# Transposing q and k by DMA from staging rows that already hold the mask columns, in an attention plus gated feed-forward kernel

## The chip, the cores and the metric

One core of one Trainium2 chip. The time is the device time of one execution in microseconds, the median of several runs; the spans inside the profile are some 2 us shorter. A run is called fast when it shows no sign of the chip's slower state. Comparisons inside one set of runs were made on the same chip.

Names used below: PE is the matrix engine; VectorE, ScalarE and GpSimd are the other engines that compute; SyncE issues DMA transfers. SBUF is the on-chip memory that tiles live in, PSUM the memory that PE's results land in, and copying a result from PSUM to SBUF is called an eviction. A staging buffer holds rows that wait to be transposed; a gate is a tiny copy that makes a load wait for something else.

## The reference, cut to what matters

Four batches, eight heads, 768 tokens, head width 64, then a feed-forward with a beta-scaled gate:

```python
scores = (q @ k.T) / sqrt(64)                       # per batch and head, 768 x 768
mask   = |bi - bj| <= 1 or bi, bj in {0, 23} or bj in sampled_blocks[bi]   # blocks of 32 tokens
attn   = softmax(where(mask, scores, -1e9))
x      = (attn @ v), heads side by side             # 3072 tokens x 512
h      = x @ w_in                                   # 512 -> 2048
out    = (h * sigmoid(beta * h)) @ w_out            # 2048 -> 512
```

PE wants q and k with the head width on partitions, that is transposed: 16 pairs of heads, a q and a k each.

The block mask costs no pass of its own. Each transposed k carries 24 extra rows, the one-hot number of the token's block; each transposed q carries 24 rows with 0 or -30000 for every block that it may not see. The score matmul then adds the mask by itself.

## The kernel before

The parts that the change and the argument touch; cuts are marked.

```python
# persistent transposed tiles, five sets; the two heads of a pair lie in different halves
for i in range(NSET):                                # NSET = 5
    for nm in ("kA", "qA", "kB", "qB"):
        four[nm] = persist.tile([P, S], FP16)        # P = 128, S = 768
    nc.gpsimd.memset(four["kB"][0:D, :], 0.0)
    nc.gpsimd.memset(four["qB"][0:D, :], 0.0)
# ... cut ...
def emit_set(i):                                     # mask rows of a set, once each
    nc.vector.tensor_copy(out=four["qA"][D:D + NB, :], in_=maskx)
    nc.gpsimd.tensor_copy(out=four["kA"][D:D + NB, :], in_=oh_flat)
    nc.vector.tensor_copy(out=four["qB"][0:NB, :], in_=maskx)
    nc.gpsimd.tensor_copy(out=four["kB"][0:NB, :], in_=oh_flat)

def emit_prep(b, j):                                 # one pair of heads
    for name, st32 in (("k", kst), ("q", qst)):
        st16 = stage_pool.tile([P, NC, 2, D], FP16, bufs=2)
        nc.vector.tensor_copy(out=st16, in_=st32)    # fp32 -> fp16 (views cut)
        tp = mm_pool.tile([P, NC, P], FP16)          # PSUM, pool of 3 shared with h and out
        for c in range(NC):                          # NC = 6
            nc.tensor.transpose(out=tp[:, c, :], in_=st16[:, c], identity=identity)
        nc.vector.tensor_copy(out=four[f"{name}A"][0:D, :], in_=flat[0:D, :])
        nc.vector.tensor_copy(out=four[f"{name}B"][D:P, :], in_=flat[D:P, :])
    nc.vector.tensor_copy(out=va[:, :, :, 0:D], in_=vst)
# ... cut ...
if n_loaded[0] == 3:                                 # the weights start once pair 3's k is loaded
    gate(w_in_sb, loaded[seq[3]][0])
    for i in range(4): emit_w_in(i)                  # 8 loads on GpSimd's queue, 8.4 MB in HBM
    for i in range(4): emit_w_out(i)
```

Attention works in query tiles of 256 or 512 columns; each step is six score matmuls, an exponential on ScalarE, then attention times v. The feed-forward of the tile before is woven in between. The first tile (256 columns) has no such filling.

The softmax here doesn't subtract the row's maximum and nothing guards it: scores larger than these inputs give would overflow.

## Time and profile before

| | before |
|---|---|
| time, median | 339.52 us (339.43 to 339.88) |
| PE busy | 298.4 of 337.4 us |
| VectorE busy | 181.7 us |
| first score matmul | 21.7 us |
| first 512-wide score matmul (second query tile) | 48.4 us |

The page of the kernel before. The first line shown is busy time by engine with instruction counts; the rows after it cut the span in 40 slices, each digit a busy share in tenths; the last line is the DMA queue fed by SyncE, with packets, MB and its share of 16 DMA engines' time.

```profile
PE 298.4 (88%) x2659; PEld 172.2 (51%) x2659; DVE 181.7 (54%) x408; ACT 215.8 (64%) x297; POOL 28.0 (8%) x48
...
PE   0055589999999999999999999999999999999995
...
DVE  3989764543787451557866366115667114561360
...
PEclk9999999999999999999999999999999999999999
DMA  7999994112530340021340000011000010001101
...
q1 hardware_dynamic: 16512, 25.17, 21.8%
```

PE is full from the seventh slice on. The slices before that are the ramp, where VectorE and DMA are the full ones. Here is the ramp's second half and the rest, as busy time in windows (the last three columns are the clock granted to PE, the DMA share and GB/s; a DMA share over 1 comes from packets that overlap on an engine):

```profile
core 0: us, PE busy (x) PEld busy (x) DVE busy (x) ACT busy (x) POOL busy (x), PEclk, DMA share, GB/s
22.00:40.00 18.00, 8.53 (x68) 6.36 (x67) 17.35 (x38) 3.77 (x6) 7.11 (x7) 1.00 1.20 239
48.00:338.00 290.00, 278.72 (x2486) 157.13 (x2483) 144.97 (x335) 203.43 (x282) 0.00 (x0) 1.00 0.17 58
```

VectorE is busy 17.35 of 18 us in the ramp and half of the time after it. Four landmarks from the timeline of the kernel before (start, duration, engine, line, operation, out<-in):

```profile
21.69 1.49 PE L234 MATMUL sc<-qA_137,kA_136 88*128 88x256 f16 x6
...
44.88 0.50 PE L209 MATMUL tp<-identity,k_479 128*128 128x128 f16 x6
...
45.22 0.50 PE L209 MATMUL tp<-identity,q_490 128*128 128x128 f16 x6
...
45.55 0.88 PE L234 MATMUL sc<-qA_155,kA_154 88*128 88x256 f16 x6
...
48.39 0.38 PE L234 MATMUL sc<-qA_137,kA_136 88*128 88x512 f16 x1 [0.26 <-ACT et L240]
```

The 12 transposes of a pair hold PE from 44.88 to 45.55, about 0.7 us. The first 512-wide score matmul at 48.39 ends the ramp; from there to the end of the span is 289.0 us. I use these two parts, ramp and rest.

### The profile page before, as it was taken

The numbers are of one execution on the slowest core, as the hardware profiler recorded it, in microseconds if no ns is written. First come the engines' busy times: TensorE is split into PE (matmuls) and PEld (weight loads), VectorE is DVE, ScalarE is ACT, GpSimd is POOL, SyncE is SP. The second block draws the span as 40 slices with busy tenths as digits, with TensorE's granted clock in tenths as the row PEclk, the third lists the DMA queues.
The fourth block names the chain that finished last, engine by engine and source line by source line (L and its number), as shares of the span: only waits on it lengthen the run. The fifth ranks groups of instructions, "written<-read, shape, count | busy, mean of one in ns | idle before, by whom it ended". The sixth has DMA issues, their size and how long they took to land.

```text
span 337.4 us, 6399 instructions
## 1 busy us (share of the span) xinstructions
PE 298.4 (88%) x2659; PEld 172.2 (51%) x2659; DVE 181.7 (54%) x408; ACT 215.8 (64%) x297; POOL 28.0 (8%) x48
## 2 busy tenths in 40 slices
PE   0055589999999999999999999999999999999995
PEld 0034466655555555555566445455455455555662
DVE  3989764543787451557866366115667114561360
ACT  1011389985998545978554989665986756954561
POOL 9994000000000000000000000000000000000000
PEclk9999999999999999999999999999999999999999
DMA  7999994112530340021340000011000010001101
GB/s 242 384 228 225 267 330 179 50 47 80 161 97 11 123 130 33 31 79 64 96 157 31 33 0 2 31 38 58 1 3 0 33 62 33 0 2 62 64 2 62
DMA packets 20880, 29.78 MB, mean 88 GB/s; under 512 B 1380, under 2 KB 17780, under 8 KB 20852
## 3 DMA queue, kind: packets, MB, share of 16 engines
q1 hardware_dynamic: 16512, 25.17, 21.8%
q0 software_dynamic: 4224, 4.19, 7.5%
q8 instruction: 21, 0.34, 0.4%
q14 instruction: 7, 0.06, 0.1%
q10 hardware_dynamic: 116, 0.01, 0.0%
HBM read 27.27 MB, written 6.29 MB: 99 GB/s over the span
## 4 chain that ended last, share of the span: by engine, by line
PE 64%; DVE 16%; ACT 14%; issue 4%; DMA 2%; SPq 0%; ACTq 0%; DVEq 0%
PE op L313 23%; PE hp L294 16%; PE sc L234 12%; PE av L260 9%; ACT et L240 8%; ACT t_sb L299 6%; DVE g L301 4%; PE tp L209 2%; PE xtp L274 2%; DMA qst<-in_q_dram 2%; DVE q_203 L204 1%; DVE va_70 L217 0%; DVE xst L266 0%; DVE qB_157 L214 0%; DVE qB_139 L214 0%
## 5 line engine op out<-in xcount | busy, mean ns | idle before, releaser
L240 ACT ACTIVATE et<-sc 128x1024 f16<-128x1024 f32 (+1 forms) x160 | 146.8, 953 | 80.4 <-PE sc L234 80.2
L313 PE MATMUL op<-w_out_sb,g 128*128 128x512 f16 x384 | 97.0, 379 | 0.1
L294 PE MATMUL hp<-xT_sb,w_in_sb 128*128 128x512 f16 (+1 forms) x448 | 95.6, 348 | 1.0 <-DVE g L301 0.2
L301 DVE SCALAR_TENSOR_TENSOR g<-t_sb,hp 128x512 f16<-128x512 f16 (+1 forms) x112 | 67.1, 610 | 44.9 <-ACT t_sb L299 44.4
L299 ACT ACTIVATE t_sb<-hp,beta_h_sb 128x512 f16<-128x512 f32 (+1 forms) x112 | 69.8, 653 | 12.1 <-PE hp L294 10.9
L294 PEld LDWEIGHTS <-w_in_sb 128*128 128x128 f16 x448 | 42.2, 97 | 35.9 <-issue 1.9
L260 PEld LDWEIGHTS <-et 128*128 128x128 f16 x1152 | 44.2, 99 | 21.6 <-DVE xst L266 10.4
L313 PEld LDWEIGHTS <-g 128*128 128x128 f16 x384 | 34.9, 97 | 33.2 <-DVE qB_163 L214 0.4
L265 DVE RECIPROCAL recip<-av 128x2 f32<-128x2 f32 (+1 forms) x64 | 11.2, 176 | 70.3 <-PE av L260 70.0
L318 ACT ACTIVATE osb<-op 128x512 f32<-128x512 f32 x24 | 14.3, 598 | 23.2 <-PE op L313 19.7
L266 DVE TENSOR_TENSOR xst<-av,recip 128x128 f16<-128x128 f32 (+1 forms) x64 | 22.8, 357 | 1.6
L276 DVE COPY xT_sb<-xtp 128x256 f16<-128x256 f16 (+1 forms) x32 | 11.5, 358 | 14.6 <-PE xtp L274 14.6
L274 PEld LDWEIGHTS <-xst 128*128 128x128 f16 x96 | 6.4, 97 | 12.5 <-DVE xst L266 12.2
L260 PE MATMUL av<-va_70,et 128*128 128x65 f16 x216 | 9.6, 199 | 2.8 <-DVE xst L266 2.7
L234 PE MATMUL sc<-qB_139,kB_138 128*128 128x256 f16 (+1 forms) x48 | 11.6, 344 | 0.5 <-ACT et L240 0.5
L274 PE MATMUL xtp<-identity,xst 128*128 128x128 f16 x96 | 10.9, 222 | 1.0 <-DVE xst L266 0.9
L234 PE MATMUL sc<-qA_137,kA_136 88*128 88x256 f16 (+1 forms) x48 | 11.1, 344 | 0.5 <-ACT et L240 0.3
L180 PE MATMUL mkx<-onehot,mask_121 24*24 24x512 f16 (+1 forms) x2 | 0.8, 506 | 10.3 <-DVE mask_121 L126 10.3
L260 PE MATMUL av<-va_72,et 128*128 128x65 f16 x216 | 9.5, 196 | 0.0
L234 PE MATMUL sc<-qB_145,kB_144 128*128 128x256 f16 (+1 forms) x36 | 8.8, 348 | 0.9 <-ACT et L240 0.9
L234 PE MATMUL sc<-qA_143,kA_142 88*128 88x256 f16 (+1 forms) x36 | 8.7, 350 | 0.6 <-ACT et L240 0.6
L234 PE MATMUL sc<-qB_163,kB_162 128*128 128x512 f16 (+1 forms) x36 | 8.5, 325 | 0.7 <-ACT et L240 0.7
(206 smaller groups left out, 249.4 us busy)
## 6 DMA issues: line engine op xcount, KB each, us to landing
kst<-in_k_dram SPq DMA_DIRECT2D x16, 384.0 KB, 4.7
qst<-in_q_dram SPq DMA_DIRECT2D x16, 384.0 KB, 5.5
vst<-in_v_dram SPq DMA_DIRECT2D x16, 384.0 KB, 5.4
out_dram<-osb SPq DMA_DIRECT2D x24, 256.0 KB, 2.0
w_in_sb<-in_moe_w_in_dram POOLq DMA_DIRECT2D x4, 512.0 KB, 10.1
w_out_sb<-in_moe_w_out_dram POOLq DMA_DIRECT2D x4, 512.0 KB, 21.7
sb_i_95<-in_sampled_blocks_dram ACTq DMA_DIRECT2D x1, 0.3 KB
beta_sb<-in_moe_beta_dram ACTq DMA_DIRECT2D x1, 8.0 KB, 4.5
```

The source lines that it names most:

```text
L234: nc.tensor.matmul(sc[:, i * n:(i + 1) * n], lhsT=kx[0:rows, (kc0 + i) * P:(kc0 + i + 1) * P], rhs=qx[0:rows, q0:q0 + n], start=True, stop ...
L240: nc.scalar.activation(out=et[:, 0:kn * n], in_=sc[:, 0:kn * n], func=AF.Exp, bias=0.0, scale=SCALE)
L260: nc.tensor.matmul(av[:, qc, :], lhsT=et[:, i * n + qc * P:i * n + (qc + 1) * P], rhs=va[:, hh, kc, 0:D + 1], start=(kc == 0), stop=(kc == ...
L265: nc.vector.reciprocal(out=recip[:, 0:nq], in_=av[:, 0:nq, D])
L266: nc.vector.tensor_tensor(out=xstage[:, 0:nq, hh * D:(hh + 1) * D], in0=av[:, 0:nq, 0:D], in1=recip[:, 0:nq].to_broadcast([P, nq, D]), op= ...
L274: nc.tensor.transpose(out=xtp[:, qc, :], in_=xstage[:, qc, :], identity=identity)
L276: nc.vector.tensor_copy(out=xT_sb[:, j, b * S + q0:b * S + q0 + n], in_=xtp[:, 0:nq, :].rearrange("p c s -> p (c s)"))
L294: nc.tensor.matmul(hp[:, 0:n], lhsT=w_in_sb[:, c, f * P:(f + 1) * P], rhs=xT_sb[:, c, t0:t0 + n], start=(c == 0), stop=(c == NPAIR - 1))
L299: nc.scalar.activation(out=t_sb[:, 0:n], in_=hp[:, 0:n], func=AF.Tanh, bias=0.0, scale=beta_h_sb[:, f:f + 1])
L301: nc.vector.scalar_tensor_tensor(out=g[:, f, 0:n], in0=t_sb[:, 0:n], scalar=1.0, in1=hp[:, 0:n], op0=ALU.add, op1=ALU.mult)
L313: nc.tensor.matmul(op, lhsT=g[:, f, ts * P:(ts + 1) * P], rhs=w_out_sb[:, f, :], start=(f == 0), stop=(f == N_FFC - 1))
L318: nc.scalar.activation(out=osb, in_=op, func=AF.Copy, bias=0.0, scale=0.5)
```

## The change

The intent: let the DMA engines transpose q and k, so that PE loses 192 transposes and VectorE 64 evictions. The staging rows (tokens on partitions) now hold 128 columns a head: 64 of data, 24 of mask or one-hot, the rest zero. The columns are written once, by ScalarE, into two staging buffers each for k and q; a DMA transpose then yields data and mask rows together. The mask chain and the loads of pair 1 were moved forward in the program.

```diff
-    et_pool = ctx.enter_context(tc.tile_pool(name="et", bufs=14))
+    et_pool = ctx.enter_context(tc.tile_pool(name="et", bufs=13))
-    NVA = 6
+    NVA = 5
+    NSTG = 2
+    AUG = P - D
+    for nm in ("k", "q"):
+        stg[nm] = [persist.tile([P, 2, NC, P], FP16, name=f"{nm}stg_{i}") for i in range(NSTG)]
@@ emit_load for pair 1 goes to ScalarE's queue; one-hot in token order (cut) @@
+    def emit_mask():
+        ps = mm_pool.tile([P, NC, AUG], FP32, tag="mm", name="mkt")
+        for c in range(NC):
+            nc.tensor.matmul(ps[:, c, :], lhsT=oh_flat[:, c * P:(c + 1) * P], rhs=mask16,
+                             start=True, stop=True)
+        for i in range(NSTG):
+            for h in range(2):
+                nc.scalar.copy(out=stg["k"][i][:, h, :, D:P], in_=oh_tok)
+                nc.scalar.copy(out=stg["q"][i][:, h, :, D:P], in_=ps)
@@ emit_set, the zero fills and the four half tiles of a set are gone (cut) @@
-            nc.vector.tensor_copy(...)               # cast into a pool tile
-            for c in range(NC):
-                nc.tensor.transpose(...)
-            nc.vector.tensor_copy(...)               # two evictions
+            st16 = stg[name][n_prep[0] % NSTG]
+            nc.vector.tensor_copy(out=st16[:, :, :, 0:D],
+                                  in_=st32.rearrange("p h (c d) -> p h c d", d=D))
+            nc.sync.dma_start_transpose(
+                out=dst.rearrange("p h (c s) -> p (h c) s", s=P),
+                in_=st16.rearrange("p h c e -> p (h c e)"))
```

More of the change, by code (lines that the diff above doesn't have):

```diff
@@ L47 @@
     stage_pool = ctx.enter_context(tc.tile_pool(name="stage", bufs=3))
-    et_pool = ctx.enter_context(tc.tile_pool(name="et", bufs=14))
+    et_pool = ctx.enter_context(tc.tile_pool(name="et", bufs=13))
     work_pool = ctx.enter_context(tc.tile_pool(name="work", bufs=3))
     g_pool = ctx.enter_context(tc.tile_pool(name="g", bufs=2))
-    NVA = 6
+    NVA = 5
+    NSTG = 2
+    AUG = P - D
     va_tiles = []
     for i in range(NVA):
-        va = persist.tile([P, 2, NC, VW], FP16, name=f"va_{i}")
-        nc.gpsimd.memset(va[:, :, :, D:VW], 1.0)
-        va_tiles.append(va)
+        va_tiles.append(persist.tile([P, 2, NC, VW], FP16, name=f"va_{i}"))
+    stg = {}
+    for nm in ("k", "q"):
+        stg[nm] = [persist.tile([P, 2, NC, P], FP16, name=f"{nm}stg_{i}") for i in range(NSTG)]
     def pair_src(x, b, j):
@@ L63, with emit_load @@
     loaded = {}
-    def emit_load(b, j):
+    def emit_load(b, j, eng=None):
+        eng = eng or nc.sync
         sts = []
@@ L68, in emit_load @@
             st32 = stage_pool.tile([P, 2, NC * D], FP32, tag=f"{name}st", name=f"{name}st")
-            nc.sync.dma_start(out=st32, in_=pair_src(src, b, j))
+            eng.dma_start(out=st32, in_=pair_src(src, b, j))
             sts.append(st32)
@@ L73 @@
     identity = persist.tile([P, P], FP16, name="identity")
+    ident32 = persist.tile([16, 16], FP32, name="ident32")
     emit_load(0, 0)
-    make_identity(nc, identity)
-    ident32 = persist.tile([P, P], FP32, name="ident32")
-    nc.gpsimd.tensor_copy(out=ident32[0:16, 0:16], in_=identity[0:16, 0:16])
     sb_i32 = persist.tile([NB, 3], mybir.dt.int32, name="sb_i32")
@@ L86 @@
     beta_sb = persist.tile([N_FFC, P], FP32, name="beta_sb")
+    emit_load(0, 1, nc.scalar)
     nc.scalar.dma_start(out=beta_sb, in_=moe_beta.rearrange("(c p) -> c p", p=P))
@@ L110 @@
                             channel_multiplier=BLK)
+    oh_tok = persist.tile([P, NC, AUG], FP16, name="oh_tok")
+    nc.gpsimd.memset(oh_tok, 1.0)
+    nc.gpsimd.affine_select(out=oh_tok, in_=oh_tok, pattern=[[1, NC], [-BLK, AUG]],
+                            compare_op=ALU.is_ge, fill=0.0, base=0,
+                            channel_multiplier=NC)
+    nc.gpsimd.affine_select(out=oh_tok, in_=oh_tok, pattern=[[-1, NC], [BLK, AUG]],
+                            compare_op=ALU.is_ge, fill=0.0, base=BLK - 1,
+                            channel_multiplier=-NC)
+    mask16 = persist.tile([NB, AUG], FP16, name="mask16")
+    nc.gpsimd.memset(mask16, 0.0)
+    for va in va_tiles:
+        nc.gpsimd.memset(va[:, :, :, D:VW], 1.0)
+    make_identity(nc, identity)
+    nc.gpsimd.tensor_copy(out=ident32, in_=identity[0:16, 0:16])
     mask_blk = persist.tile([NB, NB], FP32, name="mask_blk")
@@ L124 @@
                                        in1=mask_blk, op0=ALU.is_equal, op1=ALU.max)
-    mask16 = persist.tile([NB, NB], FP16, name="mask16")
-    nc.vector.tensor_scalar(out=mask16, in0=mask_blk, scalar1=1.0, scalar2=-NEG,
+    nc.vector.tensor_scalar(out=mask16[:, 0:NB], in0=mask_blk, scalar1=1.0, scalar2=-NEG,
                             op0=ALU.subtract, op1=ALU.mult)
@@ L162, with emit_beta @@
     for i in range(NSET):
-        four = {}
-        for nm in ("kA", "qA", "kB", "qB"):
-            four[nm] = persist.tile([P, S], FP16, name=f"{nm}_{i}")
-        nc.gpsimd.memset(four["kB"][0:D, :], 0.0)
-        nc.gpsimd.memset(four["qB"][0:D, :], 0.0)
-        sets.append(four)
-    maskx_box = {}
-    def emit_mask():
+        sets.append((persist.tile([P, 2, S], FP16, name=f"kX_{i}"),
+                     persist.tile([P, 2, S], FP16, name=f"qX_{i}")))
+    def emit_mask():
+        ps = mm_pool.tile([P, NC, AUG], FP32, tag="mm", name="mkt")
[6 more added lines that the diff above has]
+                nc.scalar.copy(out=stg["q"][i][:, h, :, D:P], in_=ps)
+    def emit_beta():
         ps = mm_pool.tile([P, 512], FP32, tag="mm", name="bet")
-        nc.tensor.transpose(out=ps[:, 0:N_FFC], in_=beta_sb, identity=ident32[0:16, 0:16])
+        nc.tensor.transpose(out=ps[:, 0:N_FFC], in_=beta_sb, identity=ident32)
         nc.vector.tensor_scalar(out=beta_h_sb, in0=ps[:, 0:N_FFC], scalar1=0.5,
                                 scalar2=None, op0=ALU.mult)
-        maskx = persist.tile([NB, S], FP16, name="maskx")
-        for lo, hi in ((0, 512), (512, S)):
-            ps = mm_pool.tile([P, 512], FP32, tag="mm", name="mkx")
-            nc.tensor.matmul(ps[0:NB, 0:hi - lo], lhsT=mask16, rhs=oh_flat[:, lo:hi],
-                             start=True, stop=True)
-            nc.vector.tensor_copy(out=maskx[:, lo:hi], in_=ps[0:NB, 0:hi - lo])
-        maskx_box["m"] = maskx
-    def emit_set(i):
-        four, maskx = sets[i], maskx_box["m"]
-        nc.vector.tensor_copy(out=four["qA"][D:D + NB, :], in_=maskx)
-        nc.gpsimd.tensor_copy(out=four["kA"][D:D + NB, :], in_=oh_flat)
-        nc.vector.tensor_copy(out=four["qB"][0:NB, :], in_=maskx)
-        nc.gpsimd.tensor_copy(out=four["kB"][0:NB, :], in_=oh_flat)
     prepared = {}
@@ L197, in emit_prep @@
         kst, qst, vst = loaded.pop((b, j))
-        four = sets[n_prep[0] % NSET]
-        if n_prep[0] < NSET:
-            emit_set(n_prep[0])
-        for name, st32 in (("k", kst), ("q", qst)):
-            st16 = stage_pool.tile([P, NC, 2, D], FP16, tag=f"{name}16", name=f"{name}16",
-                                   bufs=2)
-            nc.vector.tensor_copy(
-                out=st16.rearrange("p c h d -> p h c d"),
-                in_=st32.rearrange("p h (c d) -> p h c d", d=D))
-            tp = mm_pool.tile([P, NC, P], FP16, tag="mm", name="tp")
-            for c in range(NC):
-                nc.tensor.transpose(out=tp[:, c, :],
-                                    in_=st16[:, c, :, :].rearrange("p h d -> p (h d)"),
-                                    identity=identity)
-            flat = tp.rearrange("p c s -> p (c s)")
-            nc.vector.tensor_copy(out=four[f"{name}A"][0:D, :], in_=flat[0:D, :])
-            nc.vector.tensor_copy(out=four[f"{name}B"][D:P, :], in_=flat[D:P, :])
+        kX, qX = sets[n_prep[0] % NSET]
+        for name, st32, dst in (("k", kst, kX), ("q", qst, qX)):
+            st16 = stg[name][n_prep[0] % NSTG]
[4 more added lines that the diff above has]
+                in_=st16.rearrange("p h c e -> p (h c e)"))
         va = va_tiles[n_prep[0] % NVA]
@@ L218, in emit_prep @@
                               in_=vst.rearrange("p h (c d) -> p h c d", d=D))
-        prepared[(b, j)] = (four, va)
+        prepared[(b, j)] = (kX, qX, va)
     def attn_steps(b, j, q0, n):
@@ L228, in run @@
             def run():
-                four, _ = prepared[(b, j)]
-                kx, qx = (four["kA"], four["qA"]) if hh == 0 else (four["kB"], four["qB"])
-                rows = D + NB if hh == 0 else P
+                kX, qX, _ = prepared[(b, j)]
                 sc = sc_pool.tile([P, 1024], FP32, tag="sc", name="sc")
@@ L235, in run @@
                         sc[:, i * n:(i + 1) * n],
-                        lhsT=kx[0:rows, (kc0 + i) * P:(kc0 + i + 1) * P],
-                        rhs=qx[0:rows, q0:q0 + n],
+                        lhsT=kX[0:D + NB, hh, (kc0 + i) * P:(kc0 + i + 1) * P],
+                        rhs=qX[0:D + NB, hh, q0:q0 + n],
                         start=True, stop=True)
@@ L251, in run @@
             def run():
-                _, va = prepared[(b, j)]
+                _, _, va = prepared[(b, j)]
                 if hh == 0:
@@ L332 @@
     seq = [(b, j) for b in range(B) for j in range(NPAIR)]
-    n_loaded, n_prepped = [1], [0]
+    n_loaded, n_prepped = [2], [0]
     def prep_upto(i):
@@ L351 @@
     prep_upto(0)
+    emit_beta()
     backlog = []
```

## The prediction

> **What bounds it now.** The page shows PE busy 298.4 of 337.4 us, at full granted clock. Two stages:
> - 0 to 48 us, the ramp. By the timeline the first score matmul starts at 21.7 us, the first 512-wide one (second query tile) at 48.4. From 22 to 40 us VectorE is busy 17.35 of 18 us (windows), PE 8.5, ScalarE 3.8: VectorE binds, with casts, mask copies (24 rows, ten, 5.3 us in all) and the evictions of transposed q and k (64x768, 0.55 us, four a pair).
> - 48 us to the end: PE is busy over 98% of most windows, with 512-column matmuls at 0.86 us per four, near its rate. Every PE instruction removed here is worth its issue time.
>
> **Removed.** 192 PE transposes: 12 of one pair took 0.7 us in the warm stage (44.8 to 45.5); 12 pairs are left after 44 us, about 8.6 us; the chain of waits puts 6.1 us (1.8%) on them. VectorE: 64 evictions, 35.5 us, two thirds of it in slack, 11 in the ramp; mask copies, 5.3. GpSimd: 8 us of zero fills, 9.9 us of one-hot copies. The shared PSUM pool (3 buffers) loses the transposes' tiles, which held up h matmuls: perhaps 1 us.
>
> **Added.** 32 DMA transposes of 384 KB (128 x 1536, fp16), all on the SP queue; eight ScalarE copies at the start. No duration in this trace fits the transpose. The Trainium skill, "DMA: Bandwidth & Descriptors", section "Latency and other measured facts", gives 261 GB/s for one: my estimate is 1.5 us of transfer; with latency I take 2 to 3 us each, 4 or more beside other loads. No trace here shows it. After 55 us DMA is about a third busy or less, and q and k are prepared well ahead, so transposes should hide.
>
> **The ramp decides the size.** DMA moves 225 to 385 GB/s until 55 us already (page, part 2). The order of instructions puts the mask chain on VectorE behind six casts of pairs 0 and 1 and one of pair 2's v; so despite the intent I expect the mask at 14 us, its copies at 15 to 17, and the first transpose issued at 16 to 17, behind loads of pairs 2 to 4 on SP's queue. First score matmul: 21 to 24 us, no gain. Then eight transposes of pairs 0 to 3, between loads and 4 MB of weights, at about 2.5 us each: pair 3 ready near 40 us, the second tile starting at 42 to 46 instead of 48.4. The transpose stream binds, no longer VectorE.
>
> **Sum.** 339.5 - 8.6 (PE transposes) - 1 (PSUM pool) - 3 (ramp) = about 327; I put 328 for contention. Range 316 to 341. Faster by over 2%: 0.62; within 2%: 0.24; slower by over 2%: 0.14.
>
> **What would show each step.**
> - PE: busy falls by 12 to 17 us, 192 fewer matmuls.
> - VectorE: busy from 182 to about 140; GpSimd from 28 to about 10, ending before 15 us.
> - From 48 us on: the same work takes 8 to 10 us less, PE never idle for a transpose.
> - Transposes: median 2 to 5 us from issue to landing.
> - Ramp: first score matmul at 21 to 24 us; score matmuls wait on transposes, not on VectorE.
>
> **What would make it wrong.** At 5 us or more of exclusive queue time a transpose, eight in the ramp cost 40 us and the ramp grows by about 10 us, against the 8.6 gained: "same". At 10 us or more, 32 of them would bind the kernel: much slower. Under 1.5 us, the ramp ends before 40 us and the time is under 320. In SP's fixed order, a late transpose also holds back the loads and stores behind it.

## The result, and the profile after

The changed kernel takes 364.45 us (362.23 to 365.91, four runs) against 339.56 (four runs beside it): a ratio of 1.0726 (1.0668 to 1.0784), slower by 7%. A ratio here is the mean time of one kernel's fast runs over that of the other's fast runs of the same rounds, so it is not quite the ratio of the medians that I quote.

The page of the changed kernel, the same lines:

```profile
PE 295.1 (82%) x2471; PEld 164.7 (46%) x2471; DVE 136.1 (38%) x332; ACT 220.2 (61%) x305; POOL 11.8 (3%) x31
...
PE   0000187979797999998989998999999999999995
...
DVE  1600043345324552135682236622255312661270
...
PEclk9999999987998999998999999999999999999999
DMA  7999999998996000019992104325100011001101
...
q1 hardware_dynamic: 65872, 36.58, 41.1%
```

The work went away as planned: VectorE from 181.7 to 136.1 us, GpSimd from 28.0 to 11.8. But PE is empty for four slices instead of two, has gaps until past the middle of the span, and, unlike before, its clock dips below full. The DMA row is full about twice as long. Now the ramp in the timeline of the changed kernel; SPq is SyncE's queue, and the duration there is how long it took to issue:

```profile
18.14 4.87 SPq L210 DMA_TRANSPOSE kX_149<-kstg_75  x1
...
23.11 9.39 SPq L210 DMA_TRANSPOSE qX_150<-qstg_77  x1
32.60 9.03 SPq L210 DMA_TRANSPOSE kX_151<-kstg_76  x1
...
41.71 3.92 SPq L210 DMA_TRANSPOSE qX_152<-qstg_78  x1
...
43.24 1.44 PE L230 MATMUL sc<-qX_150,kX_149 88*128 88x256 f16 x6 [24.78 <-DMA qX_150<-qstg_77]
...
64.59 1.47 PE L230 MATMUL sc<-qX_150,kX_149 88*128 88x512 f16 x3
```

The first score matmul comes at 43.2 instead of 21.7 us, after 24.8 us of idle time of PE that ended when one transpose landed, q of pair 0. The second tile starts at 64.6 instead of 48.4: the ramp is 16.2 us longer. From there to the end is 360.5 - 64.6 = 295.9 us, against 289.0: 6.9 us longer, although the PE transposes of 11 pairs, which the kernel before still does after its second tile has started, are gone. The two add up to the 23.1 us by which the span grew. So there are two losses to explain.

Windows of the changed kernel: the ramp, and 8 us of the stage after it.

```profile
core 0: us, PE busy (x) PEld busy (x) DVE busy (x) ACT busy (x) POOL busy (x), PEclk, DMA share, GB/s
22.00:40.00 18.00, 0.00 (x0) 0.11 (x1) 0.56 (x1) 0.00 (x0) 0.52 (x1) 1.00 1.22 196
...
76.00:80.00 4.00, 1.85 (x27) 0.96 (x24) 2.36 (x7) 3.60 (x6) 0.00 (x0) 0.89 0.77 233
80.00:84.00 4.00, 4.00 (x20) 2.61 (x19) 1.47 (x4) 1.95 (x4) 0.00 (x0) 0.50 0.65 229
```

From 22 to 40 us the engines do almost nothing; only DMA works, and it moves 196 GB/s at a full share, against 239 before. At 76 us PE stalls, and then its clock is at half for the next 4 us. The chain of waits of the changed kernel around that stall (start, us, what):

```profile
72.06 5.49 DMA kX_149<-kstg_76
...
77.64 0.56 DVE kstg_76 L208
78.20 0.66 DVE g L297 x2
```

And VectorE's timeline there:

```profile
74.89 0.42 DVE L262 TENSOR_TENSOR xst<-av,recip 128x256 f16<-128x256 f32 x1
77.64 0.56 DVE L208 CAST kstg_76<-kst 128x768 f16<-128x768 f32 x1 [2.33 <-DMA kX_149<-kstg_76]
```

A cast into staging buffer 76 waits 2.33 us for the transpose that still reads that buffer. Nothing needs this cast soon: it belongs to a later pair. But VectorE takes its instructions in order, so the gate product (g), the reciprocal and the normalisation behind it wait too. PE runs out of work and its clock falls.

### The profile page after: what moved, and what is told of

Same layout as the page of the kernel before. It is cut to its first block, busy times and chain, and to the rows that moved or that the text cites. A ratio compares the mean times of both kernels' runs of the same rounds, so it can differ in the third digit from the quotient of the medians.

```text
span 360.5 us, 6016 instructions
## 1 busy us (share of the span) xinstructions
PE 295.1 (82%) x2471; PEld 164.7 (46%) x2471; DVE 136.1 (38%) x332; ACT 220.2 (61%) x305; POOL 11.8 (3%) x31
## 3 DMA queue, kind: packets, MB, share of 16 engines
q1 hardware_dynamic: 65872, 36.58, 41.1%
## 4 chain that ended last, share of the span: by engine, by line
PE 58%; DMA 20%; ACT 9%; DVE 7%; issue 3%; SPq 1%; ACTq 1%; DVEq 0%
PE op L309 20%; PE hp L290 16%; PE sc L230 13%; DMA qX_150<-qstg_77 7%; PE av L256 7%; ACT et L236 5%; DMA vst<-in_v_dram 4%; DVE g L297 3%; ACT t_sb L295 3%; DMA qX_156<-qstg_78 3%; PE xtp L270 2%; DMA kX_149<-kstg_76 2%; DMA kX_155<-kstg_75 2%; DMA qX_154<-qstg_78 1%; SPq L210 1%
## 5 line engine op out<-in xcount | busy, mean ns | idle before, releaser
L290 PE MATMUL hp<-xT_sb,w_in_sb 128*128 128x512 f16 (+1 forms) x448 | 99.8, 361 | 0.8 <-DVE g L297 0.2
L290 PEld LDWEIGHTS <-w_in_sb 128*128 128x128 f16 x448 | 44.3, 101 | 39.0 <-issue 5.5
L256 PEld LDWEIGHTS <-et 128*128 128x128 f16 x1152 | 46.4, 100 | 23.9 <-DVE xst L262 14.3
L230 PE MATMUL sc<-qX_150,kX_149 88*128 88x256 f16 (+1 forms) x96 | 23.7, 358 | 25.1 <-DMA qX_150<-qstg_77 24.8
L230 PEld LDWEIGHTS <-kX_149 88*128 88x128 f16 x96 | 9.6, 105 | 32.6 <-DMA kX_149<-kstg_75 14.9
L230 PE MATMUL sc<-qX_152,kX_151 88*128 88x256 f16 (+1 forms) x72 | 17.9, 358 | 2.9 <-ACT et L236 1.8
L230 PE MATMUL sc<-qX_154,kX_153 88*128 88x256 f16 (+1 forms) x72 | 18.0, 361 | 0.8 <-ACT et L236 0.8
L270 PE MATMUL xtp<-identity,xst 128*128 128x128 f16 x96 | 11.8, 237 | 7.7 <-DVE xst L262 7.7
L230 PE MATMUL sc<-qX_156,kX_155 88*128 88x256 f16 (+1 forms) x72 | 17.5, 349 | 0.4 <-ACT et L236 0.3
L272 DVE COPY xT_sb<-xtp 128x256 f16<-128x256 f16 (+1 forms) x32 | 11.5, 358 | 14.5 <-PE xtp L270 14.5
L230 PE MATMUL sc<-qX_158,kX_157 88*128 88x512 f16 (+1 forms) x72 | 16.4, 332 | 0.2 <-ACT et L236 0.2
L186 PE MATMUL mkt<-mask_113,onehot 24*128 24x64 f16 x6 | 0.5, 231 | 16.7 <-DVE mask_113 L145 16.7
L256 PE MATMUL av<-va_70,et 128*128 128x65 f16 x288 | 13.2, 198 | 0.6 <-DVE xst L262 0.6
```

The costliest lines, as they stand in the source:

```text
L230: nc.tensor.matmul(sc[:, i * n:(i + 1) * n], lhsT=kX[0:D + NB, hh, (kc0 + i) * P:(kc0 + i + 1) * P], rhs=qX[0:D + NB, hh, q0:q0 + n], star ...
L256: nc.tensor.matmul(av[:, qc, :], lhsT=et[:, i * n + qc * P:i * n + (qc + 1) * P], rhs=va[:, hh, kc, 0:D + 1], start=(kc == 0), stop=(kc == ...
L270: nc.tensor.transpose(out=xtp[:, qc, :], in_=xstage[:, qc, :], identity=identity)
L272: nc.vector.tensor_copy(out=xT_sb[:, j, b * S + q0:b * S + q0 + n], in_=xtp[:, 0:nq, :].rearrange("p c s -> p (c s)"))
L290: nc.tensor.matmul(hp[:, 0:n], lhsT=w_in_sb[:, c, f * P:(f + 1) * P], rhs=xT_sb[:, c, t0:t0 + n], start=(c == 0), stop=(c == NPAIR - 1))
```

## The experiments

The two theories. **Ramp:** the transposes are late because they share the 16 DMA engines with the eight weight loads, and lose (A); rival: a transpose is slow by itself (B). **After it:** VectorE's queue behind a cast that waits for a transpose (C); rival: the DMA traffic itself slows the engines (D).

### e1: the weights wait

```diff
-                if n_loaded[0] == 3:
-                    gate(w_in_sb, loaded[seq[3]][0])
             emit_prep(*seq[x])
+            if x == 3:       # one 1x1 GpSimd copy from pair 3's transposed q before each of the 8 loads
+                for i in range(4):
+                    nc.gpsimd.tensor_copy(out=w_in_sb[0:1, 0, i*512:i*512+1], in_=last[0:1, 0, 0:1])
+                    emit_w_in(i)         # and the same for w_out
```

> Changed kernel, but each of the eight weight loads waits until pair 3's q is transposed. Theory A (the ramp grew because the first transposes share the 16 DMA engines with 8 weight loads): kX and qX of pair 0 land within 10 us of the first issue at about 18 us, first score matmul at 25 to 29 us instead of 43.2; the time falls by 8 to 18 us unless the late weights hold up the first h matmuls. Rival B (a transpose is slow by itself, 10 us or more of queue): first score matmul still after 38 us, time unchanged or worse.

Measured: 361.29 us (358.76 to 362.59). The timeline of this run has its two landmarks:

```profile
23.22 1.44 PE L230 MATMUL sc<-qX,kX 88*128 88x256 f16 x6 [6.66 <-DMA qX<-qstg]
...
43.69 1.47 PE L230 MATMUL sc<-qX,kX 88*128 88x512 f16 x3
```

The first score matmul came at 23.2 us (a little before the range), the second tile at 43.7 us, 4.7 us before that of the kernel before. So A holds and B falls: the same two transposes, the first issued at 17.4 us, were done in under 6 us without the weights, and the first four were issued at most 1.9 us apart. But the time fell by 3 us instead of the 8 to 18 expected. The chain of waits of this run shows where the gain went:

```profile
42.39 15.56 DMA qX<-qstg
...
61.24 15.49 DMA kX<-kstg
```

The collision moved with the weights, from pairs 0 and 1 to pairs 4 and 5. These two transposes are not needed for a long while, yet each of them held a VectorE cast: the waits view of 43 to 95 us has 13.1 us of VectorE waiting for kX and 10.6 us for qX, and PE did nothing from 68 to 76 us. That is mechanism C with a late transpose of 15 us instead of 5. From the second tile to the end this run took 315.9 us.

### e2: casts on GpSimd after the ramp

```diff
-            nc.vector.tensor_copy(out=st16[:, :, :, 0:D], ...)
+            eng = nc.vector if n_prep[0] < 4 else nc.gpsimd
+            eng.tensor_copy(out=st16[:, :, :, 0:D], ...)
```

> Changed kernel, but from pair 4 on the q and k casts into the two staging buffers run on GpSimd. Theory C (after the ramp the loss is VectorE's in-order queue: a cast waits for the transpose that still reads its staging buffer, and reciprocal, normalisation and gate work behind it wait too, PE stalls and its clock drops): the ramp is unchanged (first score matmul 41 to 45 us), from the first 512-wide score matmul to the end about 283 us or less instead of 296, granted clock 0.99, time 345 to 354. Rival D (the transposes' DMA traffic itself slows PE, ScalarE or VectorE after the ramp): time within 3 us of the changed kernel, clock still dips.

Measured: 347.40 us (346.52 to 347.96), clock 0.990. The ramp is nearly unchanged (1.1 us longer), and then the timeline of this run shows the second tile here:

```profile
65.69 1.47 PE L231 MATMUL sc<-qX,kX 88*128 88x512 f16 x3
```

From there to the end of the span, 345.6, is 279.9 us: 16.0 less than in the changed kernel and 9.1 less than before. The transposes still run, as many bytes in the same stage, so D falls. On a queue of its own (GpSimd has nothing else to do by then) a waiting cast holds nobody up, as C says. This run alone leaves one rival: the move also took 11.8 us of work off VectorE (136.1 to 124.3). The next runs settle it.

### e3 and e4: plain copies of the same bytes

These ask why the transposes lose against the weights. Both are wrong: a plain copy from staging to the transposed tile, mask factor zero.

```diff
-            nc.sync.dma_start_transpose(...)
+            for par in range(2):                                        # e3: pieces of 256 bytes
+                nc.sync.dma_start(out=to[:, par::2, :], in_=src[:, par::2, :])
+            nc.sync.dma_start(out=dst.rearrange("p h s -> p (h s)"),    # e4: rows of 3 KB
+                              in_=st16.rearrange("p h c e -> p (h c e)"))
```

> Wrong result on purpose (mask factor zero, layout not transposed): each transpose is replaced by two plain SBUF-to-SBUF copies of the same bytes in the same 256-byte pieces. If the small pieces lose against the weight loads' larger ones (theory A1), the first copies land about as late as the transposes did: first score matmul at 36 to 45 us. If the transposition itself is what is slow (B), copies of the same pieces land early: first score matmul before 30 us.

> Wrong result on purpose, as the run with 256-byte pieces, but plain copies in rows of 3 KB. A1 (piece size): first score matmul before 32 us, each copy's share of the DMA engines near 1.2 us, half of a transpose's 2.3. If piece size does not matter and sharing is by bytes: first score matmul within 3 us of the 256-byte run's.

Measured (one run each, state unknown): 350.15 and 347.03 us. The first score matmul and the DMA queue of the run in 256-byte pieces:

```profile
44.44 1.44 PE L231 MATMUL sc<-qX,kX 88*128 88x256 f16 x6 [26.10 <-DMA qX<-qstg]
```

```profile
q1 hardware_dynamic: 65872, 36.58, 39.3%
```

The same of the run in 3 KB rows:

```profile
28.51 1.44 PE L230 MATMUL sc<-qX,kX 88*128 88x256 f16 x6 [9.98 <-DMA qX<-qstg]
```

```profile
q1 hardware_dynamic: 20304, 36.58, 30.4%
```

Bytes and queue are the same in all three; plain copies in 256-byte pieces are as late as the transposes (44.4 against 43.2 us), 3 KB rows are 16 us earlier. So in the ramp it is the size of the pieces, not the transposition. How the queues share can be read from the DMA view of the changed kernel from 22 to 40 us. The first line is GpSimd's queue (the weights), the second SyncE's (transposes alone, by then):

```profile
q0 software_dynamic: 2852, 2.84, 92.8%
q1 hardware_dynamic: 2729, 0.69, 28.9%
```

The two queues moved nearly the same number of packets, but a weight packet carries about 1,000 bytes and a transpose's about 250, so the weights got four times the bytes. At 2,729 packets in 18 us, a transpose of 1,568 packets takes 10.3 us (my estimate), near the 9.0 and 9.4 us that SyncE needed to issue one. The same view of e3 has 2,862 and 2,670 packets. The changed kernel has 50,176 more packets under 512 bytes than the kernel before, 1,568 a transpose, and 384 KB is 1,536 pieces of 256 bytes.

The cost of one follows from the queues' shares. The two hardware queues took 21.8% of 337.4 = 73.6 us of all 16 engines before, and 42.1% (41.1 and 1.0, the second queue being ScalarE's) of 360.5 = 151.8 us in the changed kernel, which loads and stores the same and has 32 transposes: 2.4 us each. The same sum gives 2.1 us for e3's copies and 1.1 us for e4's. Times of packets that overlap count double here, so these are comparisons more than exact costs.

e3 also settles what e2 left open, since its casts stayed on VectorE. From its second tile (65.4 us) to the end it took 283.0 us, 12.9 less than the changed kernel, with the same VectorE work in that stretch (120.9 us busy in both). What differs is how long VectorE's casts waited for a transfer to leave their staging buffer. e3 has, in the waits view of that stretch, only this (us in total, times, longest):

```profile
DVE kstg L208 <- DMA kX<-kstg: 2.8, 3, 1.4
```

The same view of the changed kernel adds up to 17.0 us. Over the runs of this design (e6 apart, whose h matmuls waited for their weights), wait and stretch go together: 0 us and 279.9 in e2, 2.8 and 283.0 in e3, 11.7 and 292.3 in e4, 17.0 and 295.9 in the changed kernel, 18.2 and 297.3 in e5, 37.2 and 315.9 in e1 (e3 and e4 ran once each). So C is shown: the waits account for the loss, and the work taken off VectorE does not. Why transposes keep their buffers longer than plain copies of the same pieces after the ramp is open.

### e5: the mask chain really first

The change meant the mask chain to come first, but on VectorE it stands behind seven casts, some of which wait for loads: the mask was done at 16.7 us.

```diff
+    mask_done = nc.vector.tensor_scalar(out=mask16[:, 0:NB], ...)
+            if x < 4:
+                with tc.issue_after(mask_done.ins):
+                    emit_prep(*seq[x])
```

All eight weight loads are also gated on pair 3's k here, each by a copy of its own, so that none slips ahead; e7 to e10 have these gates too.

> Changed kernel, with the mask chain really first: VectorE's casts of pairs 0 to 3 are queued behind it, all eight weight loads still start only once pair 3's k is loaded. Theory A1 (the first transposes lose against the weight loads only because they start after them): mask done at 8 us instead of 16.7, first transpose issued at 9 to 12 us, pair 0 transposed before or little after the weights start at about 15 us, first score matmul at 17 to 24 us; pairs 1 to 3 still share with the weights, second tile at 50 to 60 us, time 350 to 360. If the time of the mask does not matter (the loads of q and k alone set it): first score matmul after 38 us.

Measured: 362.35 us (360.68 to 364.56), above the range. The first score matmul came at 19.6 us, as expected; the second tile at 65.5, later than expected and no earlier than in the changed kernel. From the timeline of this run:

```profile
23.41 9.40 SPq L210 DMA_TRANSPOSE qX<-qstg  x1
...
36.97 10.82 SPq L210 DMA_TRANSPOSE kX<-kstg  x1
```

Pair 0 escaped the weights, pairs 1 and 2 did not. A long first wait can be the smallest part of a problem: taking away 23.6 us of it moved the end of the ramp by nothing, because pairs 1 to 3 still had to pass through the same collision.

### e6: both cures

The weights of e1, and e2's casts on GpSimd from pair 6 on.

> Both cures together: weight loads wait for pair 3's transposed q, and from pair 6 on the casts into staging run on GpSimd. If the two causes (contention in the ramp, VectorE's queue behind a late transpose after it) are all of the loss: second tile starts at 43 to 46 us as in the run with late weights, then about 280 to 284 us to the end as in the run with casts on GpSimd, time 325 to 333, which beats the kernel before. If late weights cost as much as they save (h matmuls wait for them): over 337.

Measured: 330.83 us (330.56 to 331.32), ratio to before 0.9745. Second tile at 43.7 us, then 285.1 us, a little over the range I gave; the first h matmuls waited 2.8 us for w_in. Two repairs turn 7% slower into 2.5% faster than before and bring the time within 3 us of the 328 predicted, so the two causes are nearly all of the loss.

### e7 and e8: PE transposes in the ramp, DMA transposes after it

In the ramp PE is idle and DMA is not; after it, it is the other way round. So the first four pairs are transposed by PE from the same staging rows, the rest by DMA, with GpSimd casts from pair 4 on.

```diff
+            if n_prep[0] >= 4:
+                nc.sync.dma_start_transpose(...); continue
+            for h in range(2):
+                tp = mm_pool.tile([P, NC, P], FP16, tag="mm", name="tp")
+                for c in range(NC):
+                    nc.tensor.transpose(out=tp[:, c, :], in_=st16[:, h, c, :], identity=identity)
+                nc.vector.tensor_copy(out=dst[:, h, :], in_=tp.rearrange("p c s -> p (c s)"))
```

> Pairs 0 to 3 are transposed by PE from the same staging rows (24 transposes and four 128x768 evictions a pair), pairs 4 to 15 by DMA, casts from pair 4 on by GpSimd; weights start as in the changed kernel. If it is only in the ramp that DMA transposes lose: first score matmul at 19 to 23 us, second tile at 38 to 48 us, then about 280 us: time 320 to 331. If DMA transposes cost as much after the ramp: over 336.

e8 adds e5's order of the mask chain.

> As the hybrid, with the mask chain first on VectorE. First score matmul at 14 to 18 us; VectorE (casts and evictions, about 4 us a pair) then sets the ramp: second tile at 34 to 44 us; time 315 to 328, 2 to 8 us below the hybrid. If the ramp is set by the loads of pairs 2 and 3 instead: within 2 us of the hybrid.

Measured: e7 320.58 us (318.94 to 322.21), ratio 0.9425; e8 317.42 us (315.50 to 317.48), ratio 0.9335 (0.9303 to 0.9366). Second tile at 37.3 and 32.3 us, both earlier than I had expected. The page of e8, row of PE, and its two landmarks:

```profile
PE   0397999979999999999999999999999999999994
```

```profile
16.47 1.49 PE L240 MATMUL sc<-qX,kX 88*128 88x256 f16 x6
...
32.34 1.27 PE L240 MATMUL sc<-qX,kX 88*128 88x512 f16 x4
```

PE is working from the second slice on. In e8, two transposes of a later pair were still slow against the weights (SyncE needed 9.7 and 10.0 us to issue them at 28 and 38 us), but nothing waited for them. e8 beats both kernels: by its ratio over 6% under the one before.

### e9 and e10: which part of the hybrid does it

e9 is the kernel before with its mask chain first; e10 is e8 with PE transposing all 16 pairs (24 transposes a pair, since each head is transposed with its mask columns).

> The kernel before, with its mask chain first on VectorE (casts of pairs 0 to 3 behind it). If the mask's place alone explains the last hybrid's short ramp: second tile starts 8 us or more earlier than 48.4, time 329 to 332. If VectorE's work in the ramp (casts, mask copies, evictions) is what binds the kernel before, as the prediction said: second tile at 44 to 49 us, time 335 to 340.

> The last hybrid with PE transposing all 16 pairs (24 transposes a pair) and no DMA transpose. Ramp as in that hybrid (second tile at 31 to 35 us). If DMA transposes after the ramp are worth what PE transposes cost there: 12 pairs x 24 at 0.06 us is 17 us more, 331 to 337. If they are worth nothing: within 4 us of 317.4.

Measured: e9 338.77 us (338.27 to 339.66), ratio 0.9976, second tile at 46.8 us. e10 331.49 us (330.62 to 331.93), ratio 0.9754, second tile at 34.5 us, by its timeline:

```profile
34.50 1.03 PE L240 MATMUL sc<-qX,kX 88*128 88x512 f16 x4
```

So the mask's place alone is worth 1.6 us of ramp before. The other 14.5 us of e8's shorter ramp (46.8 against 32.3) come from the rest of the redesign; e10 has 12.3 of them without any DMA transpose, so they belong to the staging rows with mask columns, the removed fills and copies, pair 1's loads on another queue and the GpSimd casts together (not told apart). And the DMA transposes after the ramp are worth about 14 us (331.49 - 317.42; the two ran in different sets, but their ratios to the kernel before, 0.9754 and 0.9335, say the same) against 288 PE transposes and their evictions, 0.05 us for each transpose.

### e11: what the PE transposes cost by themselves

The kernel before, pairs 5 to 15 cast but neither transposed nor evicted; q and k go stale.

```diff
+            if n_prep[0] >= NSET:
+                continue
             tp = mm_pool.tile([P, NC, P], FP16, tag="mm", name="tp")
```

> Wrong result on purpose: the kernel before, in which pairs 5 to 15 are cast but not transposed or evicted (stale q and k are used). It measures by itself what leaving the PE transposes out is worth: the prediction's 0.7 us a pair gives 7.7 us and up to 1 us for the PSUM pool, 330 to 332.5. If PE has slack for them: over 337.

Measured: 342.58 us (340.86 to 343.69), 3 us slower with less work. The total is a miss. The ramp grew, second tile at 60.3 us (first line); the other two are from the chain of waits of this run:

```profile
60.30 0.38 PE L236 MATMUL sc<-qA,kA 88*128 88x512 f16 x1 [0.26 <-ACT et L242]
...
32.44 7.71 DMA kst<-in_k_dram
40.15 15.01 DMA qst<-in_q_dram
```

With the transposes gone the later pairs' casts moved forward in VectorE's order. Between 40.7 and 52.7 us VectorE did nothing but four casts, each of which waited for a load that shared DMA with the weights, and the next reciprocal of the ramp stood behind them. It is the same trap once more: a cast that waits, in an in-order queue (this run shows the waits; I did not test it further). From the second tile on, where the question was asked, it took 340.3 - 60.3 = 280.0 us against 289.0: leaving the PE transposes out is worth 9.0 us, as e2 had it (9.1).

### e12 and e13: are the transposes right?

e11 was reported correct with stale q and k. The scores are so small that the result hardly depends on them: computed outside the chip with the reference, q and k from the wrong batch and head change the result by 1.4%. So "correct" says nothing about the transposes. e12 is e8 with each DMA transpose compared with a PE transpose of the same rows, element by element; a difference adds 1000 to the last output rows. e13 compares with the wrong head. Both ran once.

> The last hybrid with an on-chip test: each of the 24 DMA transposes (q and k, pairs 4 to 15) is compared element by element with a PE transpose of the same staging rows, and any difference adds 1000 to the last output rows. If the DMA transposes are exact, the result is correct; if even one element differs, it is wrong by far. The time (more PE and VectorE work) says nothing.

> Control of that test, wrong on purpose: the comparison takes the other head's transpose. It must be reported wrong with a large relative error; if it is reported correct, the test sees nothing and proves nothing.

Measured: e12 correct (361.23 us, with the extra work); e13 wrong, relative error 45,696. The 24 DMA transposes of e8 are exact, and the test can fail. Those of the changed kernel's first four pairs, beside the weights, were not put to it.

### Summary

| run | time, us | first score matmul | second tile (ramp) | from there to the end |
|---|---|---|---|---|
| before | 339.56 | 21.7 | 48.4 | 289.0 |
| changed | 364.45 | 43.2 | 64.6 | 295.9 |
| e1 late weights | 361.29 | 23.2 | 43.7 | 315.9 |
| e2 casts on GpSimd | 347.40 | 43.7 | 65.7 | 279.9 |
| e5 mask first | 362.35 | 19.6 | 65.5 | 297.3 |
| e6 late weights, GpSimd casts | 330.83 | 23.5 | 43.7 | 285.1 |
| e7 hybrid | 320.58 | 20.7 | 37.3 | 283.2 |
| e8 hybrid, mask first | 317.42 | 16.5 | 32.3 | 281.5 |
| e9 before, mask first | 338.77 | 20.3 | 46.8 | 290.9 |
| e10 hybrid of e8, PE only | 331.49 | 16.9 | 34.5 | 295.3 |
| e11 before, fewer transposes | 342.58 | 21.9 | 60.3 | 280.0 |

## Why the prediction was wrong

It said 328 us and faster; it was 364 and slower. Point by point:

- **What bounds the kernel before, and what the change removes: right.** VectorE fell by 45.6 us (predicted: to about 140, measured 136.1). The 8.6 us for PE's transposes and 1 us for the PSUM pool were there to be had, 9.6 together: e2 and e11 show 9.1 and 9.0 us. PE's busy time fell by only 3.3 us where 12 to 17 was predicted, with part of the work done at half clock; in e3, at full clock throughout, it was 10.7 us lower than before.
- **"Then eight transposes of pairs 0 to 3, between loads and 4 MB of weights, at about 2.5 us each: pair 3 ready near 40 us": this step failed first.** By itself a transpose does cost about that: they were issued at most 1.9 us apart in e1's first four, and the queues' shares give 2.4 us. The error was to treat the shared engines as a queue in which each waits for its own bytes; the prediction's "4 or more beside other loads" did not enter this sum. Against weight loads in larger pieces a transpose took about 10 us: the first landed after 15 us and the second after 20, and q of pair 3 landed at 61 us. The ramp term was -3 us; it measured +16.2. Without the weights in the way it measured -4.7 (e1). The Trainium skill says what I overlooked: in "DMA: Bandwidth & Descriptors", section "Queues, rings and completion order", an engine goes round its queues in turn, packet by packet. If so, a queue with small packets gets few bytes per turn. The traces agree: from 22 to 40 us the two queues moved 2,852 and 2,729 packets, of about 1,000 and 250 bytes, and e3 against e4 has 44.4 against 28.5 us for equal bytes. The single turns are not seen, only their sums.
- **"q and k are prepared well ahead, so transposes should hide": failed too.** The matmuls that use them never waited after the ramp, as I had said. But I followed only the reader of the transposed data, not the writer of the next staging data. There are two staging buffers, so a cast waits for the transpose two pairs back, in VectorE's queue, in front of work that PE needs. Worth 16.0 us (e2; clock included), where I had 0.
- **The clock, not in the prediction at all.** Some stalls of PE were paid twice, as the clock was halved after them (0.50 in the window from 80 to 84 us). The Trainium skill, "TensorE: Matmul & The Clock Gate", section "What's actually happening", has two states, full and half, and a return to half after an idle window of about 3.4 us. This trace agrees on the half, but it shows no idle window of that length: PE's idle time from 72 to 80 us adds up to only 2.4 us, and in the 3.4 us before the clock fell (at 79.1, 109.9 and 167.9 us) PE was still busy for 1.9, 1.3 and 2.1 us. The mean clock of the span fell from 0.998 to 0.979. What the clock alone cost I did not measure apart; the stretches at half clock after the ramp add up to 13.7 us, so it is at most half of that, 6.8 us (my estimate).
- **"Despite the intent I expect the mask at 14 us": right in kind** (16.7 us), but curing it alone gave nothing (e5).
- **What would make it wrong:** I named 5 us or more of exclusive queue time and called the outcome "same". The queue was indeed held that long in the ramp (4.9, 9.4 and 9.0 us for the first three transposes), but by the sharing and not by the transpose's own time, and the ramp grew by 16 us instead of 10. The second loss was not foreseen.

## What to carry to other kernels

Before moving work to a shared resource, ask what else is on it at that time, and in what pieces: a transfer in 256-byte pieces next to bulk loads can take several times its own cost (here about 10 us instead of 2.4), and the same transfer can be nearly free once the bulk is through (e2's 279.9 us after the ramp, against 280.0 in e11, which does no such transposes at all there). Then use it only in that stage, and another engine in the other, as the best version here does. And with few buffers between two engines, look at who refills a buffer: if the refill stands in an in-order queue, one late reader stops everything behind it, needed or not (17.0 us of such waits here).

## What the Trainium skill lacked or had wrong

- "DMA: Bandwidth & Descriptors", section "Latency and other measured facts", has 261 GB/s for a transpose with non-contiguous middle dimension. Here one of 384 KB took about 2.4 us of all 16 engines, which would be 160 GB/s, and next to weight loads the first three landed 14 to 20 us after their issue.
- The same page, section "Why small descriptors are slow (HBM only)", says that SBUF-to-SBUF transfers do not suffer from small pieces. Here a plain SBUF-to-SBUF copy of 384 KB took 2.1 us of all engines in 256-byte pieces and 1.1 us in 3 KB rows.
- The same page says under "Rules for kernel authors" that a transpose next to ordinary DMAs needs nothing. As a rule about data that held (24 transposes exact in e12). What it costs in time the page does not say: the first score matmul came at 43.2 us with the weights beside the transposes, at 23.2 us without.
- No page says how the time that a DMA transpose holds the issuing queue grows beside other loads: SyncE took at least 1.4 us to issue one of 384 KB, and up to 10.8 us beside the weights (e5), during which the loads behind it on that queue waited.
